# One PSUM ring for both layers of a two-mixture network, and attention scores of two heads in the two halves of the array's rows

## The chip, the cores and the metric

One NeuronCore of a Trainium2 chip runs the whole program. Its engines work side by side, each in the order of its own instruction stream: TensorE (PE, with its weight loads as PEld), VectorE (DVE), ScalarE (ACT), GpSimd (POOL) and SyncE (SP), which issues most DMAs. The metric is the device time of one execution in microseconds (us); lower is better.

## What is computed

The reference has three stages, one after the other.

```python
# 1. linear attention with decay: 4 batches, 8 heads, 768 tokens, 48 values a head
for t in range(S):
    cur = einsum('bhd,bhe->bhde', u[None] * k_t, v_t)
    y[:, :, t] = einsum('bhd,bhde->bhe', r_t, state + cur)
    state = w[None, :, :, None] * state + einsum('bhd,bhe->bhde', k_t, v_t)
# x: 3072 tokens of 384 values
# 2. first mixture, 4 experts, each token passes all of them (p: normalised weights)
out = sum over e of p[:, e:e+1] * (relu(x @ w1[e]) @ w2[e])      # 384 -> 1024 -> 384
# 3. second mixture, 8 experts; each token goes to one, by a greedy assignment over all
#    3072 x 8 gate logits, largest first, at most 384 tokens an expert
out[mask_e] = relu(x[mask_e] @ w1[e]) @ w2[e]
```

Everything is float32 in and out.

## The kernel before

**Precision.** A float32 product of the mixtures is made as three products in the type fp32r: each factor is written as a high part and a low part (ACT casts the high part, POOL or DVE subtracts it to get the low part), and high by high, high by low and low by high are added in PSUM.

**Units.** The first mixture runs in 32 units: four batches, four experts, two blocks of 384 tokens. A unit is `up` and then `down`. `up` has eight steps f; each makes nine products of 128x128 by 128x384 (L672, L674, L676) into one PSUM buffer, then ACT writes relu of it as the high part of h (L680) and DVE the low part (L681). `down` has three steps i of 24 products each (L693, L695, L697) and one DVE eviction (L939 or L941). `up` takes its buffers from a ring of two named l1, `down` from a ring of two named l2, and all else from a ring of four named at: eight buffers in all. The second mixture uses the same `up` and `down`, one expert after another, while the search for the next expert's tokens runs on DVE and PE in between.

**Attention chunks.** A chunk is 128 tokens of one batch, all eight heads; there are 24. The first six are done ahead of the units and in the first one, with plain float32 products for the scores (L556: one product for a head, 48 rows of the array, rows 0 to 47 for one head of a pair and 64 to 111 for the other). The other 18 are done one to a unit, in units 1 to 6 of each group of eight, and have `split_scores` set. Chunk work is a list of steps in `queue`. `tick`, called three times in a step of `up` and eight times in a step of `down`, takes a step from the queue each third time, so one step of the list follows each step f of `up`. The order for these 18 chunks before: mul (POOL, L492), k_parts (DVE cast L533, POOL difference L534), r_parts for the even heads and r_parts for the odd ones (each a DVE cast L539 and a DVE difference L540 on 64 partitions), pre (POOL: L498, L502, L506), pre2 (DVE reduction cc, L517, which needs L502; POOL L523), scores of the first two pairs (L549 to L551), att (scores of the other two pairs, then two DVE maskings, L562), yy (products L579 and L583, then DVE L590), state (L600) and tr (L616). The last three fall into `down`.

**How the scores of a pair are made.** Rb holds r of a pair of heads in a block-diagonal form: 256 columns, the even head's r in rows 0 to 63 of the first 128 columns, the odd head's in rows 64 to 127 of the last 128, zeros elsewhere. So one product over all 128 rows with 256 columns gives the scores of both heads, and three of them make a pair. The zeros are written once, at the start (L643).

**Which unit loads what.** In units of block 1, w1 of the next expert is split beside `up`, two parts at odd f; in units of block 0, w2, one part at each f (ACT L658, then POOL L659). Every unit with a chunk has one or the other. All of these share ACT's and POOL's order with the chunk's steps.

Of the kernel before, what the change touches and what calls it, by code (L numbers as in the profile page):

```python
# [8 lines left out]
F32 = mybir.dt.float32  # L9
# [8 lines left out]
class Route:  # L18
    """Greedy assignment, one expert filled per phase; tokens lie [128, NT]."""

# [7 lines left out]
    def consts(self):  # L28
        """Steps."""
        nc, tile, NT, E, NC = self.nc, self.tile, self.NT, self.E, self.NC  # L30
        steps = []
# [25 lines left out]
        for l, sh in enumerate(self.shift):  # L57
            v.tensor_scalar(self.G[:, l], gi, sh, None, op0=OP.logical_shift_left)
        # thresholds of the first digit, as float bits
        self.thr0 = tile([128, self.width[0] - 1], I32, "thr0")  # L60
# [3 lines left out]
        v.tensor_tensor(self.thr0, self.thr0, first, op=OP.bitwise_xor)  # L64
        # the worth of a digit, for each expert
        d = iota([E, E], "W0", F32, [[1, E]], mult=-1)
# [17 lines left out]
        self.tt = iota([128, NT, 16], "tt", BF, [[1, NT], [0, 16]])  # L84
        # rep[(v,a), (b,a')] = (a == a') * (1 if v == 0 else 128)
        r = iota([32, 128], "repi", I32, [[1, 128]], mult=-1, base=32)
# [7 lines left out]
        v.tensor_scalar(self.rep, self.rep, pf, None, op0=OP.mult)  # L94
        # bm[(b,a), (k,b')] = (b == b')
        b = iota([128, NC // 8, 8], "bmi", I32, [[0, NC // 8], [-16, 8]], mult=1)
# [3 lines left out]
        self.m = tile([128, NT], F32, "m")  # L100
        # two tiles of tokens make one product: their experts in columns from 0 and from 32
        self.ch2 = tile([128, NT // 2, 2, 32], BF, "ch")
# [8 lines left out]
    def phase(self, last, done, split=None):  # L111
        """Two lists of steps; done(idx [128, cap/128] int32, ev [128, 1] int32) is called when both are known."""
        nc, tile, pst, NT, E, NC = self.nc, self.tile, self.pst, self.NT, self.E, self.NC
# [81 lines left out]
        def rest():  # L195
            # every token left goes to the expert left
            v.tensor_reduce(m, L, axis=AX.X, op=OP.max)
            fl = tile([128, 2, NT], F32, "fl")
            v.memset(fl[:, 1], 0.0)
            v.tensor_scalar(fl[:, 0], m, -1e29, None, op0=OP.is_ge)  # L200
            scan(fl)
            s["ev"] = self.left
# [75 lines left out]

        # Each step with its time on the tensor engine and the time until the next step's operands are there.
        # The second list makes the row numbers and may run beside the next phase's search.  # L280
        tail = [(spread, 0, 1.2), (weigh, 0, 0.6), (gather, 0.78, 0.2), (index, 0.23, 0.35)]
# [13 lines left out]
def rwkv_moe_moe(ctx, tc, A, out):  # L295
# [14 lines left out]

    # The chunked form scales by powers of the decays up to the 128th, both ways; decays with which those
    # could leave the range of float32 take the step by step form instead.
    wcol = const("wcol", [128, 4], A["w"])
# [32 lines left out]
    with tc.tile_pool(name="psum0", bufs=1, space=bass.MemoryType.PSUM) as psum, tc.manual_schedule():  # L346
# [10 lines left out]
        nc.gpsimd.iota(jp, pattern=[[1, 128]], base=0, channel_multiplier=-1)  # L357
        # the tensor engine's clock rises while it is busy
        for _ in range(22):
# [5 lines left out]

        # tp[0][i] = w^(i - 64), tp[1][j] = w^(63 - j)
        def scan(p):
# [34 lines left out]
def main(ctx, tc, A, out, C, stepwise):  # L402
# [28 lines left out]
    def step_by_step():  # L431
        """x, token after token, to memory: partition (quarter of the values, b, h), state [keys, 12 values]."""
        T = 4
# [44 lines left out]

    # ---- attention
    st = {}  # L480
# [4 lines left out]
    def attn_steps(ck, detail=False):  # L485
# [42 lines left out]

        # Both factors of the scores as sums of two parts that one pass carries exactly;
        # r of a pair of heads lies apart, so that one product makes both heads' scores.  # L530
        def k_parts():
# [3 lines left out]

        def r_parts(s):
            t, n = ld[ck]
            q, cs = slice(64 * s, 64 * s + 64), slice(128 * s, 128 * s + 128)
            nc.vector.tensor_copy(Rb[q, 0, :, cs], t[q, 0])  # L539
            nc.vector.tensor_sub(Rb[q, 1, :, cs], t[q, 0], Rb[q, 0, :, cs].bitcast(F32))  # L540

        def scores(p0, p1):
            t, n = ld[ck]
            if p0 == 0:
                ps[ck] = [psum.tile([128, 4, 128], F32, name="at", bufs=4) for _ in range(2)]
            if split_scores:
                for p in range(p0, p1):
                    o = ps[ck][p // 2][:, 2 * (p % 2):2 * (p % 2) + 2, :]
                    nc.tensor.matmul(o, Kb[:, 0, p], Rb[:, 0, p], start=True, stop=False)  # L549
                    nc.tensor.matmul(o, Kb[:, 0, p], Rb[:, 1, p], start=False, stop=False)  # L550
                    nc.tensor.matmul(o, Kb[:, 1, p], Rb[:, 0, p], start=False, stop=True)  # L551
                return
            for p in range(p0, p1):
                for s in range(2):
                    q = slice(64 * s, 64 * s + 48)
                    nc.tensor.matmul(ps[ck][s][:, p, :], t[q, 1, p, :], t[q, 0, p, :], start=True, stop=True)  # L556
# [16 lines left out]
        def y_mm():  # L573
            t, n = ld[ck]
            v = n[:, 384:768]
            y = psum.tile([128, D], F32, name="at", bufs=4)
            for p in range(4):
                if c:
                    nc.tensor.matmul(y[:, 96 * p:96 * p + 96], t[:, 0, p, :], S[ck - 1][:, p, :],  # L579
                                     start=True, stop=False)  # L580
                for s in range(2):
                    h = 2 * p + s
                    nc.tensor.matmul(y[:, 48 * h:48 * h + 48], st[ck][:, p // 2, 2 * (p % 2) + s, :] if split_scores else st[ck][:, s, p, :],  # L583
                                     v[:, 48 * h:48 * h + 48],
                                     start=not c, stop=bool(s) or not c)
            st[ck] = y
# [46 lines left out]
        if not split_scores:  # L633
            return [lambda: (mul(nc.vector), pre()), pre2, lambda: scores(0, 2), att, yy, state, tr]
        return [lambda: mul(nc.gpsimd), k_parts, lambda: r_parts(0), lambda: r_parts(1), pre, pre2, lambda: scores(0, 2), att, yy, state, tr]

    if not stepwise:
        Rb = at.tile([128, 2, 4, 256], F32R, name="Rb")
        Kb = at.tile([128, 2, 4, 128], F32R, name="Kb")
        for s in range(2):  # L640
            q, cs = slice(64 * s, 64 * s + 64), slice(128 - 128 * s, 256 - 128 * s)
            for a in range(2):
                nc.scalar.activation(Rb[q, a, :, cs], C["zero"][q, :, None].to_broadcast([64, 4, 128]), AF.Copy)  # L643

    # ---- weights
    W1, W2 = {}, {}
# [14 lines left out]

    # ---- one pass of one expert over 384 tokens
    def up(xT, c0, after1, before1, tick, tick1=lambda: None, place=None, H=None):
        H = [] if H is None else H
        for f in range(FB):
            before1(f)
            p = psum.tile([128, D], F32, name="l1", bufs=2)
            w = W1[f]
# [18 lines left out]
    def down(H, evict, tick, tick1=lambda: None):  # L687
        for i in range(3):
            ts = slice(128 * i, 128 * i + 128)
            p = psum.tile([128, D], F32, name="l2", bufs=2)  # L690
            for f in range(FB):
# [13 lines left out]
    def dots(a, to):  # L705
        """a [128, D] with each column of the gate, to to [128, E2]."""
        def lg(e):
# [4 lines left out]

    # The logits of the last tokens don't wait for their rows: what the last expert adds to them is
    # h @ (W2 @ gate), so the search for the first expert to fill runs beside the products h @ W2.
    late, hv, gated = [], [], {}
# [88 lines left out]

    # first weights and first chunks
    def consts_in():
# [13 lines left out]
    else:  # L820
# [8 lines left out]
        def warm(n):  # L829
            p = psum.tile([128, 128], F32, name="l1", bufs=2)  # L830
            b = C["busy"].to_broadcast([128, 128])
            for _ in range(n):
                nc.tensor.matmul(p, b, b, start=True, stop=True)
# [158 lines left out]
    while lq:  # L992
        lq.pop(0)()
    # ---- second mixture: one expert after the other, in the order in which they fill
    search, number = [], []
# [5 lines left out]
    def start_job(idx, ev):  # L1001
# [4 lines left out]
        def load(which, src, q):  # L1006
            t = wk.tile([128, 2, D], F32, name="raw", bufs=4)
            d = nc.sync.dma_start(t, src[bass.ds(e, 1), :, 768 * q:768 * q + 768].rearrange("o p n -> p (o n)"))
            if jb["n"] == 0 and which == 1 and q == 2:
                # the rows, waited for, pass before the weights that aren't needed yet  # L1010
                tc.add_manual_dep(d.ins, jb["rows"].ins.name,
# [81 lines left out]
    def keep_warm(n):  # L1093
        p = psum.tile([128, 128], F32, name="l1", bufs=2)
        for _ in range(n):
            nc.tensor.matmul(p, route.tri, route.tri, start=True, stop=True)
# [125 lines left out]
```

## Time and profile before

| what | value |
|---|---|
| time, median of 3 runs | 1343.05 us (1341.25 to 1346.93) |
| profiled execution, span | 1348.0 us (no other time is given for it) |
| PE busy | 1257.2 us, 93% of the span |
| PEld busy | 1196.1 us, 89% |
| DVE busy | 756.8 us, 56% |
| ACT busy | 336.9 us, 25% |
| POOL busy | 579.1 us, 43% |
| HBM traffic | 83 GB/s over the span |

The span runs from the first to the last instruction of one profiled execution. Busy times of PE are those of pipelined products, so a product's listed duration is longer than the distance between two of them. The profiled execution is 0.4% above the median of the runs.

### The profile page before, as it was taken

To read this page: it belongs to the slowest core of one execution; us is meant where nothing else is said; L and a number is where in the kernel's file an instruction comes from. 1 tells how busy PE (TensorE), PEld (TensorE's weight loads), DVE (VectorE), ACT (ScalarE), POOL (GpSimd) and SP (SyncE) were. 2 spreads that over 40 slices of the span, in tenths; PEclk is the share of its full clock that TensorE was granted. 3 is DMA by queue.
4 is the path that set the end of the run, shared out by engine and by line. 5 is a ranking of instruction groups with operands and counts; after the bars stand their busy time and mean duration, and the time that the engine had idled before them with its cause. 6 is when DMAs were issued, how large, how long until landed. Compare 5 with 4: busy or idle time off the path is not lost.

```text
span 1348.0 us, 20834 instructions
## 1 busy us (share of the span) xinstructions
PE 1257.2 (93%) x7988; PEld 1196.1 (89%) x7988; DVE 756.8 (56%) x1891; ACT 336.9 (25%) x738; POOL 579.1 (43%) x557
## 2 busy tenths in 40 slices
PE   9999999999999999999999999999997798788897
PEld 8999999999999999999989999999986677666797
DVE  6644444465444446544444663877567778767621
ACT  1322222212222221122222113222303223323252
POOL 5565444402555550055555203332205545555583
PEclk6999999999999999999999999999997999989999
DMA  6342222112222220222221011231013423333351
GB/s 232 127 145 72 91 86 91 51 39 88 79 83 82 83 71 24 95 82 93 83 84 35 19 65 48 82 106 47 1 36 113 128 77 109 107 97 89 106 169 45
DMA packets 39469, 113.36 MB, mean 84 GB/s; under 512 B 5056, under 2 KB 9280, under 8 KB 39232
## 3 DMA queue, kind: packets, MB, share of 16 engines
q1 hardware_dynamic: 36288, 102.50, 23.3%
q0 software_dynamic: 3072, 9.44, 2.1%
q8 instruction: 64, 1.05, 0.3%
q14 instruction: 45, 0.37, 0.1%
HBM read 102.48 MB, written 9.44 MB: 83 GB/s over the span
## 4 chain that ended last, share of the span: by engine, by line
PE 73%; DVE 18%; issue 2%; POOL 2%; ACT 1%; another core or an unknown queue 1%; DMA 0%; POOLq 0%; SPq 0%; ACTq 0%
PE l L693 12%; PE l L695 11%; PE l L697 11%; PE l L672 9%; PE l L674 8%; PE l L676 8%; DVE Rb L540 4%; DVE h L681 4%; PE at L583 3%; POOL w L659 2%; DVE thr L187 2%; DVE Rb L539 2%; DVE oh L129 2%; PE at L579 2%; DVE scr L709 2%
## 5 line engine op out<-in xcount | busy, mean ns | idle before, releaser
L659 POOL TENSOR_TENSOR w<-raw,w 128x384 fp32r<-128x384 f32 x332 | 355.4, 1090 | 615.9 <-ACT w L658 603.9
L672 PE MATMUL l<-xT,w 128*128 128x384 f32 x960 | 334.4, 348 | 37.6 <-DVE h L681 37.0
L674 PE MATMUL l<-xT,w 128*128 128x384 f32 x960 | 326.9, 340 | 0.0
L676 PE MATMUL l<-xT,w 128*128 128x384 f32 x960 | 326.5, 340 | 0.0
L693 PE MATMUL l<-w,h 128*128 128x384 f32 x939 | 324.7, 346 | 0.0
L697 PE MATMUL l<-w,h 128*128 128x384 f32 x939 | 318.5, 339 | 0.0
L695 PE MATMUL l<-w,h 128*128 128x384 f32 x939 | 317.8, 338 | 0.4 <-POOL w L659 0.4
L680 ACT ACTIVATE h<-l 128x384 fp32r<-128x384 f32 x313 | 154.0, 492 | 639.2 <-PE l L676 597.7
L681 DVE SCALAR_TENSOR_TENSOR h<-l,h 128x384 fp32r<-128x384 f32 x313 | 171.2, 553 | 184.2 <-ACT h L680 183.5
L672 PEld LDWEIGHTS l<-xT,w 128*128 128x128 f32 x960 | 183.3, 191 | 56.6 <-DVE h L681 54.4
L674 PEld LDWEIGHTS l<-xT,w 128*128 128x128 f32 x960 | 183.5, 191 | 0.5
L676 PEld LDWEIGHTS l<-xT,w 128*128 128x128 f32 x960 | 183.1, 191 | 0.1
L695 PEld LDWEIGHTS l<-w,h 128*128 128x128 f32 x939 | 177.2, 189 | 1.4 <-POOL w L659 0.7
L693 PEld LDWEIGHTS l<-w,h 128*128 128x128 f32 x939 | 177.3, 189 | 1.0
L697 PEld LDWEIGHTS l<-w,h 128*128 128x128 f32 x939 | 177.1, 189 | 0.8
L658 ACT ACTIVATE w<-raw 128x384 fp32r<-128x384 f32 x336 | 163.7, 517 | 42.3 <-DMA raw<-in_v_dram 37.5
L709 DVE SCALAR_TENSOR_TENSOR scr<-acc,wg 128x384 f32<-128x384 f32 x192 | 104.8, 583 | 0.2
L941 DVE SCALAR_TENSOR_TENSOR acc<-l,dp,acc 128x384 f32<-128x384 f32 x72 | 44.4, 617 | 106.0 <-PE l L697 105.8
L1028 POOL DMA_INDIRECT acc<-x2d,idx x24 | 23.7, 987 | 81.3 <-DVE idx L269 76.3
L618 ACT ACTIVATE xT<-at 128x384 fp32r<-128x384 f32 x24 | 11.8, 492 | 180.1 <-PE at L616 173.0
L540 DVE TENSOR_TENSOR Rb<-rkT,Rb 64x512 fp32r<-64x512 f32 x36 | 52.4, 1456 | 1.2
L146 PEld LDWEIGHTS <-ch 128*40 128x40 bf16 x588 | 21.5, 104 | 34.8 <-DVE oh L129 21.4
(227 smaller groups left out, 1222.9 us busy)
## 6 DMA issues: line engine op xcount, KB each, us to landing
raw<-in_w_dram SPq DMA_DIRECT2D x104, 384.0 KB, 4.4
raw<-in_v_dram SPq DMA_DIRECT2D x64, 384.0 KB, 3.2
rkv<-in_rkv_dram SPq DMA_DIRECT2D x22, 640.0 KB, 4.1
rkT<-in_rkT_dram SPq DMA_DIRECT2D x22, 512.0 KB, 3.5
x2d<-acc SPq DMA_DIRECT2D x24, 192.0 KB, 1.8
wg<-in_wg_dram SPq DMA_DIRECT2D x1, 1536.0 KB
w2r<-in_w_dram SPq DMA_DIRECT2D x8, 192.0 KB, 3.2
xT<-in_rkv_dram SPq DMA_DIRECT2D x2, 640.0 KB, 10.4
```

Of the source, the lines that this page charges most:

```text
L540: nc.vector.tensor_sub(Rb[q, 1, :, cs], t[q, 0], Rb[q, 0, :, cs].bitcast(F32))
L658: nc.scalar.activation(w[:, 0], r, AF.Copy)
L659: engine.tensor_tensor(w[:, 1], r, w[:, 0].bitcast(F32), op=OP.subtract)
L672: nc.tensor.matmul(p, w[:, 0, ks], xh, start=(k == 0), stop=False)
L674: nc.tensor.matmul(p, w[:, 0, ks], xl, start=False, stop=False)
L676: nc.tensor.matmul(p, w[:, 1, ks], xh, start=False, stop=(k == 2))
L680: nc.scalar.activation(h[:, 0], p, AF.Relu)
L681: nc.vector.scalar_tensor_tensor(h[:, 1], p, 0.0, h[:, 0].bitcast(F32), op0=OP.max, op1=OP.subtract)
L693: nc.tensor.matmul(p, h[:, 0, ts], w[:, 0], start=(f == 0), stop=False)
L695: nc.tensor.matmul(p, h[:, 0, ts], w[:, 1], start=False, stop=False)
L697: nc.tensor.matmul(p, h[:, 1, ts], w[:, 0], start=False, stop=(f == FB - 1))
L709: nc.vector.scalar_tensor_tensor(scr[e % 2], x, 1.0, wg[:, e], op0=OP.mult, op1=OP.mult, accum_out=to[:, e:e + 1])
```

## The change

The two rings l1 and l2 become one ring mm of four buffers that `up` and `down` take from in turn. For the 18 chunks with `split_scores`, the block-diagonal form of r goes: Rb has 128 columns a pair, the even head's r in rows 0 to 63 and the odd head's in rows 64 to 127, and each head has its own products over 64 rows with 128 columns, the two heads in turn, into two PSUM buffers. The high part of r is cast by ACT, the low part made by one DVE difference over 128 partitions, and the two steps r_parts become one, so every later step of the chunk comes one step earlier. The zero fills go. The scores of even heads now lie in one tile and of odd heads in the other, as in the first six chunks. The rest of the diff takes out comments.

```diff
-        def r_parts(s):
+        def r_parts():
             t, n = ld[ck]
-            q, cs = slice(64 * s, 64 * s + 64), slice(128 * s, 128 * s + 128)
-            nc.vector.tensor_copy(Rb[q, 0, :, cs], t[q, 0])
-            nc.vector.tensor_sub(Rb[q, 1, :, cs], t[q, 0], Rb[q, 0, :, cs].bitcast(F32))
+            nc.scalar.activation(Rb[:, 0], t[:, 0], AF.Copy)
+            nc.vector.tensor_sub(Rb[:, 1], t[:, 0], Rb[:, 0].bitcast(F32))
...
             if split_scores:
                 for p in range(p0, p1):
-                    o = ps[ck][p // 2][:, 2 * (p % 2):2 * (p % 2) + 2, :]
-                    nc.tensor.matmul(o, Kb[:, 0, p], Rb[:, 0, p], start=True, stop=False)
-                    nc.tensor.matmul(o, Kb[:, 0, p], Rb[:, 1, p], start=False, stop=False)
-                    nc.tensor.matmul(o, Kb[:, 1, p], Rb[:, 0, p], start=False, stop=True)
+                    for n, (a, b) in enumerate(((0, 0), (0, 1), (1, 0))):
+                        for s in range(2):
+                            q = slice(64 * s, 64 * s + 64)
+                            nc.tensor.matmul(ps[ck][s][:, p, :], Kb[q, a, p], Rb[q, b, p], start=n == 0, stop=n == 2)
                 return
...
-                    nc.tensor.matmul(y[:, 48 * h:48 * h + 48], st[ck][:, p // 2, 2 * (p % 2) + s, :] if split_scores else st[ck][:, s, p, :],
+                    nc.tensor.matmul(y[:, 48 * h:48 * h + 48], st[ck][:, s, p, :],
...
-        return [lambda: mul(nc.gpsimd), k_parts, lambda: r_parts(0), lambda: r_parts(1), pre, pre2, lambda: scores(0, 2), att, yy, state, tr]
+        return [lambda: mul(nc.gpsimd), k_parts, r_parts, pre, pre2, lambda: scores(0, 2), att, yy, state, tr]
...
-        Rb = at.tile([128, 2, 4, 256], F32R, name="Rb")
+        Rb = at.tile([128, 2, 4, 128], F32R, name="Rb")
         Kb = at.tile([128, 2, 4, 128], F32R, name="Kb")
-        for s in range(2):
-            q, cs = slice(64 * s, 64 * s + 64), slice(128 - 128 * s, 256 - 128 * s)
-            for a in range(2):
-                nc.scalar.activation(Rb[q, a, :, cs], C["zero"][q, :, None].to_broadcast([64, 4, 128]), AF.Copy)
...
-            p = psum.tile([128, D], F32, name="l1", bufs=2)
+            p = psum.tile([128, D], F32, name="mm", bufs=4)
...
-            p = psum.tile([128, D], F32, name="l2", bufs=2)
+            p = psum.tile([128, D], F32, name="mm", bufs=4)
```

The first of the last two hunks is in `up`, the second in `down`; the two places that issue small products on constants (L830, L1094) change from l1 to mm in the same way.

## Rows read from the trace of the kernel before

**Rows 1.** Page: shares of the chain by engine, then the group of h's casts.
```profile
PE 73%; DVE 18%; issue 2%; POOL 2%; ACT 1%; another core or an unknown queue 1%; DMA 0%; POOLq 0%; SPq 0%; ACTq 0%
...
L680 ACT ACTIVATE h<-l 128x384 fp32r<-128x384 f32 x313 | 154.0, 492 | 639.2 <-PE l L676 597.7
```

**Rows 2.** Windows (length; busy us and count by engine; clock): three units; units 26 to 29.
```profile
145.51:178.35 32.84, 30.90 (x192) 30.22 (x192) 14.96 (x23) 7.73 (x17) 16.76 (x14) 1.00 0.25 85
178.35:210.44 32.09, 30.90 (x192) 30.22 (x192) 14.20 (x23) 7.74 (x17) 16.51 (x14) 1.00 0.26 86
274.47:299.43 24.96, 24.96 (x145) 24.96 (x145) 17.26 (x57) 3.94 (x8) 0.00 (x0) 1.00 0.07 25
835.35:942.30 106.95, 103.29 (x578) 99.43 (x577) 85.50 (x243) 29.73 (x66) 36.70 (x32) 1.00 0.24 74
```

**Rows 3.** Waits of PE (us, times, longest) in 75:780, 780:1008 and 1008:1348.
```profile
PE l L672 <- DVE h L681: 28.3, 36, 1.1
...
PE l L672 <- DVE h L681: 3.2, 7, 1.2
...
PE l L672 <- DVE h L681: 5.4, 5, 1.8
```

**Rows 4.** Timeline of PE (start, duration, what, [idle before <- releaser]), unit from 145.51.
```profile
153.13 0.34 PE L676 MATMUL l<-xT,w 128*128 128x384 f32 x1
154.59 0.44 PE L672 MATMUL l<-xT,w 128*128 128x384 f32 x1 [1.12 <-DVE h L681]
154.87 0.34 PE L674 MATMUL l<-xT,w 128*128 128x384 f32 x1
```

**Rows 5.** Timeline of DVE, the same unit.
```profile
151.38 0.98 DVE L539 CAST Rb<-rkT 64x512 fp32r<-64x512 f32 x1
152.40 1.67 DVE L540 TENSOR_TENSOR Rb<-rkT,Rb 64x512 fp32r<-64x512 f32 x1
153.99 0.54 DVE L681 SCALAR_TENSOR_TENSOR h<-l,h 128x384 fp32r<-128x384 f32 x1
...
158.62 0.55 DVE L517 TENSOR_REDUCE cc<-rkv 128x8 f32<-128x384 f32 x1 [0.94 <-POOL rkv L502]
...
162.43 0.68 DVE L562 TENSOR_TENSOR am<-at,mask 128x512 f32<-128x512 f32 x1
```

**Rows 6.** Groups by form (count | busy us, mean ns): the low parts of r.
```profile
L540 DVE TENSOR_TENSOR Rb<-rkT,Rb 64x512 fp32r<-64x512 f32 x36 | 52.4, 1456 | 1.2
```

**Rows 7.** Timeline of PE: scores of 256 columns, then the next product of up.
```profile
158.95 0.28 PE L549 MATMUL at<-Rb,Kb 128*128 128x256 f32 x1
...
159.66 0.34 PE L672 MATMUL l<-xT,w 128*128 128x384 f32 x1
159.84 0.34 PE L674 MATMUL l<-xT,w 128*128 128x384 f32 x1
```

**Rows 8.** Timeline of PE: float32 scores in two row halves; float32 products over all rows.
```profile
68.73 0.34 PE L697 MATMUL l<-w,h 128*128 128x384 f32 x1
69.00 0.71 PE L556 MATMUL at<-rkT 48*128 48x128 f32 x8
69.64 0.45 PE L693 MATMUL l<-w,h 128*128 128x384 f32 x1
69.92 0.34 PE L695 MATMUL l<-w,h 128*128 128x384 f32 x1
...
102.78 1.03 PE L600 MATMUL at<-rkv 128*128 128x96 f32 x8
```

**Rows 9.** The instructions of L556 (duration ns least/median/most, first and last start).
```profile
L556 PE MATMUL at<-rkT x64: 272/272/579, 6.3 to 71.9; 48*128 48x128 f32 x64
```

**Rows 10.** Timeline of POOL, the unit from 145.51.
```profile
153.48 2.60 POOL L659 TENSOR_TENSOR w<-raw,w 128x384 fp32r<-128x384 f32 x2
...
157.57 1.02 POOL L502 TENSOR_TENSOR rkv<-rkv,u_b 128x384 f32<-128x384 f32 x1
...
159.79 1.99 POOL L659 TENSOR_TENSOR w<-raw,w 128x384 fp32r<-128x384 f32 x2
```

More of the change, by code (lines that the diff above doesn't have):

```diff
@@ L829, in warm @@
         def warm(n):
-            p = psum.tile([128, 128], F32, name="l1", bufs=2)
+            p = psum.tile([128, 128], F32, name="mm", bufs=4)
             b = C["busy"].to_broadcast([128, 128])
@@ L1093, in keep_warm @@
     def keep_warm(n):
-        p = psum.tile([128, 128], F32, name="l1", bufs=2)
+        p = psum.tile([128, 128], F32, name="mm", bufs=4)
         for _ in range(n):
```

## The prediction

> **What bounds the kernel now.** I read the page's chain of waits first: PE carries 73% of the span and DVE 18% [rows 1], so whatever DVE takes off PE counts, and whatever is taken off DVE alone counts only where PE waits for it. Next the windows, one unit at a time. A unit without attention takes 24.96 us and PE is busy all of it; a unit with a chunk takes 32.84 us where it is of block 1 and 32.09 us where it is of block 0, and in both PE is busy 30.90, that is 1.9 and 1.2 us less than the unit lasts, at full clock (1.00) [rows 2]. Then PE's waits by stage: in the stretch that holds the 18 chunks, PE waited 28.3 us in 36 waits, two a chunk, and all of them are the first product of an `up` step waiting for DVE's eviction L681; later there are 7 such waits of 3.2 us and, in the second mixture, 5 of 5.4 us [rows 3].
>
> The timelines show why. The reader should see at 153.13 the last product of step f=4 and at 154.59 the first of f=5: 1.46 us where products otherwise follow each 0.17, and the next one comes 0.28 after it [rows 4]. DVE had cast and subtracted r of the even heads, from 151.38 to 154.07, before it came to L681 at 153.99 [rows 5] (spans overlap a little in DVE's pipeline). The eviction came late, the ring of two l1 buffers has room for one step only, PE stood still. The second r step does the same again three products later.
>
> **1. The ring of four.** A wait costs more than its idle time: in the rows shown 1.46-0.17 = 1.29 us and 0.28-0.17 = 0.11 for the restart, 1.40 for a listed idle of 1.12, so 0.28 more [rows 4]. For the 36 waits of the chunks that is 28.3+36x0.28 = 38.4 us [rows 3]; by unit 1.94+0.56 = 2.5 us in block 1 and 1.19+0.56 = 1.75 in block 0 [rows 2]. A step lasts nine products, 9x24.96/144 = 1.56 us [rows 2]. With two buffers, a step's buffer is needed again one step after it ends, with four, three steps, 4.7 us. An eviction needs ACT 0.49 [rows 1], DVE 0.54 [rows 5] and the 0.17 that the last product goes on, about 1.2, so the room grows from 0.4 to 3.5 us. The longest thing left in DVE's way is one r difference of 1.5 to 1.7 us [rows 5, 6]: all 38.4 us go. `down` loses nothing by sharing: its buffers come up again after three other tiles, and its eviction is one DVE instruction.
>
> **2. r in one step.** DVE loses two casts like that of 0.98 and one of two differences of 1.46 a chunk (about 3 us of its 15 in a unit [rows 2, 5, 6]); the cast goes to ACT, which is busy 7.7 us of a unit [rows 2] and whose 384-element casts take 0.49 [rows 1], so about 0.65 for 512. Price on PE: nothing, covered by the ring's 3.5 us; with the old ring it would be part of the old wait. The difference over 128 partitions instead of 64 I take at 1.46, what half the partitions cost now [rows 6]. The zero fills go from the start, where PE and DVE do other things: nothing.
>
> **3. The scores.** Before, six products of 256 columns take 159.66-158.95 = 0.71 us a block, and the product after them follows at 0.18: no loss at the edges [rows 7]. Two blocks a chunk, 36 in all. After, a block is 12 products of 128 columns on 64 rows. No fp32r product of 128 columns or on part of the rows is in this trace. The nearest row is the float32 form of the same scores in row halves: eight instructions, 0.71 us with the last one's 0.27, so 0.063 apart [rows 8, 9]. At the edges it costs: 0.27 from the product before to the first (0.10 over the usual), 0.20 from the last start to the next product, and 0.28 to the one after. From 68.73 to 69.92 is 1.19, less two usual distances 0.84, which is 8x0.063+0.34 [rows 8]. So 12x0.063+0.34 = 1.10 a block, 0.39 more than now, x36 = +13.9 us. The Trainium skill, TensorEngine Tiling (Array Packing), Tiling Modes (Key Properties), says that a change of tiling mode drains the engine; the 0.27 before and 0.20 after [rows 8] agree, and that rule alone speaks against making the block so short.
>
> Bounds of this term. Lowest: the halves share everything. 384 columns take 0.173 and 256 take 0.118 [rows 4, 7], so 128 take 0.064 in one half and 0.032 a product with two; 12x0.032 is 0.39 without edges and 0.73 with them: -11.5 to +0.7 us. High: the halves don't share weight loads. Float32 products over all rows with short columns are (1.03-0.27)/7 = 0.109 apart, if the last lasts as long as in rows 9, whatever lies behind it [rows 8]; 12x0.109+0.34 = 1.65, +34 us. Also high: a 128-column fp32r product costs what a float32 one costs, two instructions, 0.126 in shared halves: 1.85, +41 us. Highest: that, and the halves not sharing: 0.252, 3.36 a block, +95 us. I take 0.063, since the row has the same columns, the same alternation of halves and one load for each instruction. The Trainium skill, TensorE: Matmul & The Clock Gate, LDWEIGHTS (loading the stationary operand), prices a load by its columns alone, 128 over 1.2 GHz, an estimate of 107 ns for half the rows as for all; by it alone 24 loads a chunk would give about the +34 us, while Part 3 there (Packing small matmuls, The mechanism) lets loads into other rows overlap, which the 0.063 [rows 8, 9] bears out for float32.
>
> **4. Steps one earlier: a wait that moves.** pre2 now follows f=4, and its reduction cc stands in DVE's order before the evictions of f=5 and f=6 and the two maskings. cc waits for POOL's L502: in the block 1 unit that ended at 158.59 [rows 10]. Of POOL's order before it only the contention goes: two splits beside the r steps took 2.60, later ones 1.99 [rows 10], so L502 ends near 158.0. PE, without stalls: f=4's last product at 153.13, f=5 done at 154.9, scores 156.0, f=6 157.5, att 158.6, f=7 160.2; now yy comes there, not three products into `down`. DVE: cc to 158.6, eviction of f=5 to 159.1, of f=6 to 159.65, maskings of 0.68 [rows 5] to 160.95. The y products need the second masking some 0.4 after they start, at 160.6, since even and odd heads now lie in two tiles: 0.4 us of wait, 1.0 if L502 is as late as before; I take 0.5. In block 0 units one split fewer is ahead of L502 and the maskings end before PE comes: nothing, with some 2 us of cover in POOL. 9x0.5 = +4.5 us. Behind the waiting cc are evictions, which the ring covers; behind the waiting y product all of PE. Note that this wait shrinks as the scores grow and the reverse.
>
> **5. Later stages.** Units 26 to 29 take 106.95, 7.1 more than four plain units; DVE is busy 85.5 of it [rows 2]. PE's seven waits there are worth 3.2+7x0.28 = 5.2 [rows 3] and the ring should take most of the loss: between 0 and 7.1, I take 5. In the second mixture only five waits of 5.4+5x0.28 = 6.8 us [rows 3] can go, and the search runs on DVE and PE in turn, which would then wait elsewhere: 0 to 6.8, I take 2.
>
> **Sum.** -38.4+13.9+4.5-5-2 = -27.0 us on a span of 1348.0, of which nothing outside is listed; that execution lies 0.4% above the median of the runs. The terms are counted instructions and waits, so I take them off the median: 1343.05-27.0 = 1316.
>
> **The rivals.** (a) The halves share nearly all, and the scores cost 0.4 to 0.7 a block: no drain worth the name. Then PE reaches the y products up to 1.4 us earlier and waits for the same cc: about 1.1 to 1.8 us x9 = 10 to 16. -38.4+0.7+10-7 = -35 or -38.4-11.5+16-7 = -41: 1302 to 1308, I say 1306. For: float32 halves share already [rows 9]. Against: the edges in rows 8. The Trainium skill, TensorEngine Tiling (Array Packing), Overview (Theoretical Speedup), promises up to 2x for a contraction of 64 or less; by that rule this case would come.
> (b) Loads are not shared: -38.4+34-7 = -11, 1332. Or 128 columns are priced as float32: -38.4+41-7 = -4, 1339. In both the wait at the y products is gone, the scores being longer than it. For: nothing in the trace has fp32r under 256 columns. Against: 0.063 in rows 9.
> (c) The other side: priced as float32 and one half after the other, 3.36 a block: -38.4+95-7 = +50, 1393. Without the scores and the wait that they replace, the change gives 45.4 us, 1.26 a block; the scores turn it into a loss from 0.71+1.26 = 1.97 a block, 0.136 a product. Rows 8 stand at 0.063, so it takes twice that.
> (d) The change doesn't do what it says, in that cc takes the place of r: POOL a microsecond later than I think gives 2.0 us in each block 1 unit, 18 instead of 4.5, and 1330. For: POOL has no gap before L502 in block 1 [rows 10]. Against: contention goes down.
>
> **How the numbers follow.** Forecast 0.44 (1316, own range 1307 to 1326); (a) 0.10; (b) 0.28, half for each price; (c) 0.07; (d) 0.11. A measurement can tell about 0.5%, 6.7 us. Faster is below 1336.3: the forecast, (a), most of (d) (0.09), most of the first half of (b) (0.10) and the near end of the second (0.04): 0.77. Same: the rest of (d) and of (b) but 0.01, 0.15. Slower: (c) and that 0.01: 0.08. Range 1304 to 1341: (c), the far part of the second price of (b) (0.06) and the far end of (a) (0.04) are left out, under 0.2.
>
> **What would show it.** The windows: units of block 1 near 31.6 us and of block 0 near 31.1. PE's waits L672 on L681 gone before 780 us. Twelve scores 0.063 apart with 0.27 ahead of them. Waits of L583 on the masking L562, in block 1 only, under 1 us each. DVE's cc idle over 2 us for L502. Wrong would be: L672 waits left over, score products over 0.1 apart, waits of L583 in all chunks, or a second mixture that moves by more than 5 us.

## The result and the profile after

The changed kernel took 1312.03 us (median of 4 runs, 1309.02 to 1314.98) against 1344.99 for the kernel before in its 4 runs: ratio 0.9761, interval [0.9737, 0.9786]. 1316 was forecast, and faster. The profiled executions have spans of 1348.0 and 1313.2 us, 34.8 apart. Cut at the starts of units, which the first product of `up` marks:

| stretch | before | after | difference | forecast |
|---|---|---|---|---|
| start and unit 0 | 81.45 | 79.74 | -1.7 | 0 |
| units 1 to 22, all 18 chunks | 678.95 | 652.49 | -26.5 | -20.0 |
| unit 23 | 24.96 | 24.96 | 0.0 | 0 |
| units 24 to 29 | 156.94 | 153.84 | -3.1 | -5 |
| from unit 30: end of the first mixture, the second | 405.70 | 402.17 | -3.5 | -2 |

The windows of the kernel after, in the columns of [rows 2]: the two units with a chunk that answer to those rows, units 26 to 29, then units 1 to 22.

```profile
141.11:172.11 31.00, 31.00 (x205) 30.31 (x205) 12.07 (x20) 8.24 (x18) 15.83 (x14) 1.00 0.27 90
172.11:203.02 30.91, 30.91 (x204) 30.23 (x204) 11.19 (x20) 8.25 (x18) 15.69 (x14) 1.00 0.27 90
807.11:911.03 103.92, 102.05 (x578) 101.08 (x578) 87.17 (x243) 29.39 (x66) 37.31 (x32) 0.98 0.26 77
...
79.74:732.23 652.49, 652.11 (x4183) 639.36 (x4183) 280.36 (x609) 164.10 (x356) 283.20 (x261) 1.00 0.24 79
```

In a unit with a chunk PE is now busy as long as the unit lasts. DVE has about 3 us less a unit, ACT 0.5 more. The page shows the same from its chain, where PE had 73% and DVE 18% [rows 1]:

```profile
PE 79%; DVE 11%; POOL 4%; issue 4%; ACT 1%; DMA 0%; POOLq 0%; SPq 0%; DVEq 0%
```

PE's waits from 75 to 780 us, 28.3 us before [rows 3], are one row:

```profile
PE at L582 <- DVE am L561: 0.2, 1, 0.2
```

The price of the scores is in PE's timeline, to be read as [rows 7, 8] were:

```profile
88.93 0.34 PE L671 MATMUL mm<-xT,w 128*128 128x384 f32 x1
89.19 0.89 PE L550 MATMUL at<-Rb,Kb 64*128 64x128 f32 x12
90.01 0.45 PE L667 MATMUL mm<-xT,w 128*128 128x384 f32 x1
90.30 0.34 PE L669 MATMUL mm<-xT,w 128*128 128x384 f32 x1
```

Twelve products in 0.89 us with a last one of 0.27 stand (0.89-0.27)/11 = 0.056 apart on average; how they begin is read below, with the products of one half. The edges are those of the float32 scores: 0.26 ahead, 0.28 to the second product behind. The block costs 1.37 less two usual distances, 1.02 us, where it cost 0.71.

Last, the wait that was to move. DVE and PE in the unit from 141.11:

```profile
147.10 1.04 DVE L538 TENSOR_TENSOR Rb<-rkT,Rb 128x512 fp32r<-128x512 f32 x1
148.07 0.56 DVE L676 SCALAR_TENSOR_TENSOR h<-mm,h 128x384 fp32r<-128x384 f32 x1
...
153.33 0.55 DVE L517 TENSOR_REDUCE cc<-rkv 128x8 f32<-128x384 f32 x1 [3.14 <-POOL rkv L502]
...
154.73 1.28 DVE L561 TENSOR_TENSOR am<-at,mask 128x512 f32<-128x512 f32 x2
...
155.83 0.65 PE L582 MATMUL at<-rkv,am 128*128 128x48 f32 x4
```

DVE stands 3.14 us at cc, as foreseen; the second masking ends at 156.01, and PE takes it up at that moment: four L582 that last 0.57 elsewhere last 0.65. The unit of block 1 is 0.09 us longer than that of block 0, no more. It is more in the three block 1 units with the first chunk of a batch, units 1, 9 and 17: there is no state yet, so the two products L578 ahead of the y products are missing and PE comes 0.2 us sooner. In unit 1:

```profile
94.27 0.34 PE L582 MATMUL at<-rkv,am 128*128 128x48 f32 x2
94.79 1.43 PE L582 MATMUL at<-rkv,am 128*128 128x48 f32 x11 [0.18 <-DVE am L561]
```

From the first pair to the next it is 0.52 us where it is 0.18 without a wait; each of the three units loses 0.3 to 0.4 us in this way.

### The profile page after: what moved, and what is told of

It is laid out like the page before. It is cut to its first block, busy times and chain, and to the rows that moved or that the text cites. A ratio compares the mean times of both kernels' runs of the same rounds, so it can differ in the third digit from the quotient of the medians.

```text
span 1313.2 us, 21208 instructions
## 1 busy us (share of the span) xinstructions
PE 1252.3 (95%) x8204; PEld 1195.4 (91%) x8204; DVE 708.6 (54%) x1837; ACT 343.4 (26%) x752; POOL 565.1 (43%) x557
## 4 chain that ended last, share of the span: by engine, by line
PE 79%; DVE 11%; POOL 4%; issue 4%; ACT 1%; DMA 0%; POOLq 0%; SPq 0%; DVEq 0%
PE mm L688 12%; PE mm L692 12%; PE mm L690 12%; PE mm L667 11%; PE mm L669 10%; PE mm L671 10%; PE at L582 3%; POOL w L654 3%; DVE thr L187 2%; PE at L550 2%; DVE oh L129 2%; PE at L146 2%; PE at L578 2%; DVE h L676 1%; PE at L599 1%
## 5 line engine op out<-in xcount | busy, mean ns | idle before, releaser
L654 POOL TENSOR_TENSOR w<-raw,w 128x384 fp32r<-128x384 f32 x332 | 346.5, 1063 | 601.5 <-ACT w L653 586.1
L667 PE MATMUL mm<-xT,w 128*128 128x384 f32 x960 | 332.6, 346 | 0.6 <-ACT xT L1039 0.6
L669 PE MATMUL mm<-xT,w 128*128 128x384 f32 x960 | 327.1, 341 | 0.0
L671 PE MATMUL mm<-xT,w 128*128 128x384 f32 x960 | 326.3, 340 | 0.0
L688 PE MATMUL mm<-w,h 128*128 128x384 f32 x939 | 325.1, 346 | 0.8 <-ACT w L653 0.8
L675 ACT ACTIVATE h<-mm 128x384 fp32r<-128x384 f32 x313 | 153.9, 492 | 636.9 <-PE mm L671 595.2
L690 PE MATMUL mm<-w,h 128*128 128x384 f32 x939 | 318.6, 339 | 1.1 <-POOL w L654 1.1
L692 PE MATMUL mm<-w,h 128*128 128x384 f32 x939 | 318.8, 339 | 0.0
L676 DVE SCALAR_TENSOR_TENSOR h<-mm,h 128x384 fp32r<-128x384 f32 x313 | 171.9, 553 | 176.6 <-ACT h L675 176.4
L667 PEld LDWEIGHTS mm<-xT,w 128*128 128x128 f32 x960 | 184.0, 192 | 4.7 <-ACT xT L1039 1.0
L669 PEld LDWEIGHTS mm<-xT,w 128*128 128x128 f32 x960 | 183.8, 191 | 0.6
L671 PEld LDWEIGHTS mm<-xT,w 128*128 128x128 f32 x960 | 183.5, 191 | 0.1
L690 PEld LDWEIGHTS mm<-w,h 128*128 128x128 f32 x939 | 178.0, 190 | 2.3 <-POOL w L654 1.7
L688 PEld LDWEIGHTS mm<-w,h 128*128 128x128 f32 x939 | 177.7, 189 | 2.1 <-ACT w L653 1.1
L692 PEld LDWEIGHTS mm<-w,h 128*128 128x128 f32 x939 | 177.6, 189 | 0.9
L936 DVE SCALAR_TENSOR_TENSOR acc<-mm,dp,acc 128x384 f32<-128x384 f32 x72 | 44.4, 617 | 110.2 <-PE mm L692 110.1
L146 PE MATMUL at<-oh,ch 128*40 128x62 bf16 (+2 forms) x588 | 27.3, 196 | 28.3 <-DVE oh L129 22.0
L582 PE MATMUL at<-rkv,am 128*128 128x48 f32 x352 | 51.4, 273 | 0.4 <-DVE am L561 0.2
```

What stands on the lines that cost most here:

```text
L582: nc.tensor.matmul(y[:, 48 * h:48 * h + 48], st[ck][:, s, p, :], v[:, 48 * h:48 * h + 48], start=not c, stop=bool(s) or not c)
L654: engine.tensor_tensor(w[:, 1], r, w[:, 0].bitcast(F32), op=OP.subtract)
L667: nc.tensor.matmul(p, w[:, 0, ks], xh, start=(k == 0), stop=False)
L669: nc.tensor.matmul(p, w[:, 0, ks], xl, start=False, stop=False)
L671: nc.tensor.matmul(p, w[:, 1, ks], xh, start=False, stop=(k == 2))
L675: nc.scalar.activation(h[:, 0], p, AF.Relu)
```

## The experiments

Ratios are to the kernel before on the same chip, with their intervals. Runs with one number were made once, for their profile.

**The ring alone.** The kernel before, with this edit at the four places that used l1 or l2:

```diff
-            p = psum.tile([128, D], F32, name="l1", bufs=2)
+            p = psum.tile([128, D], F32, name="mm", bufs=4)
```

> The kernel before with nothing but the ring of four. Ring theory (the four buffers remove the 36 waits of 38.4 us; the new scores only cost): units with a chunk fall to 30.3 us, no wait of L672 on L681 before 780 us, and the time is 8 to 11 us below the changed kernel's, 1301 to 1304 us. Relief theory (DVE is freed by one r step, and that removes the waits): over half of the waits stay, the time is above 1325 us.

1298.46 us, 0.9673 [0.9651, 0.9695]: faster than the whole change, and lower than the 1301 to 1304 expected. The windows of two units with a chunk and of units 1 to 22:

```profile
141.85:172.33 30.48, 30.48 (x193) 30.28 (x192) 15.46 (x23) 7.73 (x17) 16.67 (x14) 1.00 0.26 92
172.33:202.62 30.29, 30.29 (x192) 30.25 (x192) 14.13 (x23) 7.74 (x17) 16.52 (x14) 1.00 0.28 91
...
81.89:723.77 641.88, 641.86 (x3967) 639.27 (x3967) 335.41 (x663) 155.04 (x338) 298.71 (x261) 1.00 0.24 81
```

DVE still does the two r steps (15.46 us of the unit, 14.96 before), and no wait of PE is listed. Units 1 to 22 are 678.95-641.88 = 37.1 us shorter: the four buffers alone take all the waits. Against the whole change, 652.49-641.88 = 10.6 us, near 36 blocks of 0.31, 11.2. (The agreement is not exact: this kernel's own block 1 units are 0.2 to 0.3 us longer than those of block 0, at the first products of a block of scores, about 2 us in all, and the change has the waits at the y products instead.)

**The change without the ring.** The changed kernel with l1 and l2 of two buffers again, the edit above backwards.

> The changed kernel with two rings of two again. Ring theory: with one step of room the evictions that now stand behind cc (3.1 us idle on DVE in block 1 units) stop PE by about 2 us in block 1 units and under 1 us in block 0 units; with 11 us of dearer scores the time is within 7 us of the kernel before, 1338 to 1350 us. Relief theory: the waits are gone with the r steps, 1315 to 1325 us.

1317.12 us, 0.9816 [0.98, 0.9833], which is what the relief theory said. Waits from 75 to 740 us, then a block 1 unit, units 26 to 29 and units 1 to 22:

```profile
PE l L667 <- DVE h L676: 3.2, 9, 0.5
```

```profile
143.36:174.71 31.35, 31.02 (x204) 30.23 (x204) 12.08 (x20) 8.24 (x18) 15.85 (x14) 1.00 0.26 89
812.10:919.19 107.09, 103.28 (x577) 99.46 (x577) 85.00 (x243) 29.70 (x66) 37.23 (x32) 1.00 0.25 75
...
81.99:737.13 655.14, 651.90 (x4184) 638.76 (x4184) 279.84 (x609) 164.09 (x356) 283.58 (x261) 1.00 0.24 79
```

Nine waits of 3.2 us in all are left of 28.3 [rows 3], all in block 1 units. So neither theory holds by itself: either half of the change takes nearly all the waits, and the second to come finds little. Two things were overlooked. The one r difference fits between two evictions (147.10 to 148.14 in the kernel after, the next eviction at 148.07). And the evictions behind cc have more room than one step: the two blocks of scores lie between f=5 and f=7, so a buffer of two is needed again 1.56+2x1.02 = 3.6 us after its step. The ring still gives 655.14-652.49 = 2.7 us here, all in block 1 units (about 0.35 in each of six; in units 1, 9 and 17, where the changed kernel waits at the y products instead, 0.0 to 0.25), and 107.09-103.92 = 3.2 in units 26 to 29.

**The old r steps under the new scores.** Two rings of two, scores in halves, and

```diff
-        def r_parts():
+        def r_parts(s):
             t, n = ld[ck]
-            nc.scalar.activation(Rb[:, 0], t[:, 0], AF.Copy)
-            nc.vector.tensor_sub(Rb[:, 1], t[:, 0], Rb[:, 0].bitcast(F32))
+            q = slice(64 * s, 64 * s + 64)
+            nc.vector.tensor_copy(Rb[q, 0], t[q, 0])
+            nc.vector.tensor_sub(Rb[q, 1], t[q, 0], Rb[q, 0].bitcast(F32))
...
-        return [lambda: mul(nc.gpsimd), k_parts, r_parts, pre, ...
+        return [lambda: mul(nc.gpsimd), k_parts, lambda: r_parts(0), lambda: r_parts(1), pre, ...
```

> Scores in row halves, but two rings of two and the two r steps of before (a DVE cast and a DVE difference each). Theory that the r steps made the waits and that their merging alone removes them: about 36 waits of L667 on L676 are back in the units with a chunk, these take 0.6 us more than before, 32.6 and 33.4 us less up to 0.5, and the time is 1.000 to 1.008 of before. Rival (the scores in halves changed the room of the evictions, and that removed the waits): no waits, 0.98 of before as with the merged step.

1355.67 us, 1.0088 [1.0065, 1.0111]. The waits from 75 to 750 us and two units:

```profile
PE l L668 <- DVE h L677: 27.0, 35, 1.1
```

```profile
146.84:180.19 33.35, 31.53 (x204) 30.16 (x204) 15.53 (x23) 7.72 (x17) 16.65 (x14) 1.00 0.25 84
180.19:212.90 32.71, 31.51 (x205) 30.19 (x204) 14.22 (x23) 7.73 (x17) 16.49 (x14) 1.00 0.26 85
```

They are back, 35 of 27.0 us (the 36th falls just behind 750 us), and the units are 0.5 to 0.6 us longer than before [rows 2]. So it is the merged step, not the halves, that does it in the kernel without the ring; and the new scores alone are a loss, of 0.9%. The merged step is three things at once, the cast moved to ACT, one difference in place of two and all later steps one earlier; no run separates them.

**Both heads' products in turn.** Three products of one head, then three of the other:

```diff
-                    for n, (a, b) in enumerate(((0, 0), (0, 1), (1, 0))):
-                        for s in range(2):
+                    for s in range(2):
+                        for n, (a, b) in enumerate(((0, 0), (0, 1), (1, 0))):
```

> The changed kernel with the three products of one head in a row, then those of the other, so that two neighbours are mostly in the same half of the rows. Theory of shared loads (neighbours in different halves overlap their weight loads, and that makes the 0.06 us distance): products in the same half stand 0.107 apart, a block grows by 0.35 to 0.5 us, the time by 8 to 18 us less up to 3 us of waits. Rival (0.064 us is what 128 columns take in any order, on the line through 256 columns at 0.118 and 384 at 0.173): distance and time unchanged.

1307.76 us, 0.9747 [0.9731, 0.9763]: no change. The block:

```profile
92.73 0.89 PE L550 MATMUL at<-Rb,Kb 64*128 64x128 f32 x12
```

That could mean that halves don't matter, or that three still pair with three. The next two tell.

**128 columns over all rows, and over one half.** The score product with `Kb[:, a, p]` and `Rb[:, b, p]` in place of `Kb[q, a, p]` and `Rb[q, b, p]`; and the changed kernel with `q = slice(0, 64)` for both heads.

> The changed kernel with every score product over all 128 rows, still 128 columns: the two heads of a pair are summed, so the scores are not the reference's; only its times count. Theory of shared halves (two products in different halves run beside each other; the kernel with the halves in turn could still pair up three with three): without halves the products stand 0.107 apart, a block takes 1.3 us or more against 1.02. Rival (128 columns take 0.056 in any rows): same distance of 0.056, a block of 0.7 to 1.0 us.

> The changed kernel with both heads' score products on rows 0 to 63 (the odd head's scores are those of the even head; only its times count). Theory of shared halves: one half has all the work, 0.107 apart, a block of 1.6 us with the edges, units 1.1 to 1.2 us longer than the changed kernel's. Rival (0.056 in any rows): unchanged units.

1324.86 and 1338.6 us. All rows first, then one half:

```profile
122.16 0.33 PE L671 MATMUL mm<-xT,w 128*128 128x384 f32 x1
122.33 1.45 PE L550 MATMUL at<-Rb,Kb 128*128 128x128 f32 x12
123.62 0.39 PE L667 MATMUL mm<-xT,w 128*128 128x384 f32 x1
123.85 0.34 PE L669 MATMUL mm<-xT,w 128*128 128x384 f32 x1
```

```profile
122.06 0.34 PE L671 MATMUL mm<-xT,w 128*128 128x384 f32 x1
122.33 1.55 PE L550 MATMUL at<-Rb,Kb 64*128 64x128 f32 x12
123.81 0.44 PE L667 MATMUL mm<-xT,w 128*128 128x384 f32 x1
124.09 0.34 PE L669 MATMUL mm<-xT,w 128*128 128x384 f32 x1
```

Over all rows the products stand (1.45-0.27)/11 = 0.107 apart on average and a block takes 1.69-0.35 = 1.34 us; in one half it is (1.55-0.27)/11 = 0.116 and 2.03-0.35 = 1.68, and the units are 1.3 to 1.4 us longer than the changed kernel's, where 1.1 to 1.2 were expected. The two averages differ by the first distance alone. From the second product on, all rows first:

```profile
122.39 1.39 PE L550 MATMUL at<-Rb,Kb 128*128 128x128 f32 x11
```

```profile
122.49 1.39 PE L550 MATMUL at<-Rb,Kb 64*128 64x128 f32 x11
```

That is (1.39-0.27)/10 = 0.11 apart in both, after a first distance of 0.06 over all rows and 0.16 in one half. So 128 columns are not free to run at 0.056 by themselves: two halves beside each other make it. The starts in the kernel with the heads in turn show how. The score products that have begun in two windows, both opened just before the block, are counted as x:

```profile
92.70:92.89 0.19, 0.16 (x2) 1.00 1.71 146
92.70:93.00 0.30, 0.27 (x4) 1.00 1.18 119
```

They begin in twos, a new two each 0.11 us, though the program has three products of one half in a row; in one half alone only one begins in that time. So three pair with three. The changed kernel's begin in twos as well. The Trainium skill, TensorE: Matmul & The Clock Gate, LDWEIGHTS (loading the stationary operand), sets 128 columns over 1.2 GHz for a load, an estimate of 107 ns; the 0.11 comes near, and Part 3 there (The mechanism), by which loads into other rows overlap, agrees with the twos. The entry of 0.27 shows only with 64 rows; over all rows it is 0.17. TensorEngine Tiling (Array Packing) of the Trainium skill, Tiling Modes (Key Properties), has a drain at a change of mode, and these entries agree.

**One block of scores.** All four pairs after f=5, the maskings where the second block was:

```diff
-        return [..., pre2, lambda: scores(0, 2), att, yy, state, tr]
+        return [..., pre2, lambda: scores(0, 4), am, yy, state, tr]
```

> The changed kernel with the scores of all four pairs in one block of 24 products after f=5, none after f=6. Theory of the edges (each block pays 0.34 us for entering and leaving the row halves, whatever its length): one block a chunk less, units 0.3 us shorter, the time 5 to 7 us less. Rival (the cost is in the products): units unchanged, the time within 2 us.

1319.16 us, 0.9762 [0.973, 0.9794], no gain; the units got longer, 31.2 us in both blocks. The block and the y products of one unit:

```profile
121.48 1.55 PE L550 MATMUL at<-Rb,Kb 64*128 64x128 f32 x24
122.96 0.44 PE L667 MATMUL mm<-xT,w 128*128 128x384 f32 x1
...
126.59 0.42 PE L582 MATMUL at<-rkv,am 128*128 128x48 f32 x2
127.19 0.42 PE L582 MATMUL at<-rkv,am 128*128 128x48 f32 x2 [0.18 <-DVE am L561]
```

The edges are what I took them for: 24 products in one block, again 0.056 apart, cost 1.68 us, 0.36 less than two of 1.02. But f=6 and f=7 now follow each other, the maskings wait for the eviction of f=6, and PE reaches them too early: 0.60 from one pair of L582 to the next and a wait at each of two maskings. The saving and 0.2 to 0.3 us more went there.

**One block, maskings at once.** The same, with `lambda: (scores(0, 4), am())` for the two steps, which also brings the y products one step earlier.

> The changed kernel with the scores of all pairs in one block and the two maskings in the same step, ahead of the eviction of f=6. Theory (one block saves 0.36 us of edges, and the one-block kernel lost it again because its y products came to the maskings too early): units of 30.55 us in block 0, 0.36 less than the changed kernel's, no wait of L582, the time 5 to 7 us under the one-block kernel in units 1 to 23. Rival (one block costs elsewhere): units stay at 31.2 us.

1329.71 us, 0.9911 [0.9883, 0.9939]: half right. A block 0 and a block 1 unit, two stretches of the latter, and the waits from 75 to 750:

```profile
177.43:208.01 30.58, 30.58 (x204) 30.23 (x204) 11.40 (x20) 8.25 (x18) 16.05 (x14) 1.00 0.28 91
208.01:243.30 35.29, 34.23 (x205) 33.59 (x204) 12.67 (x20) 8.24 (x18) 16.16 (x14) 0.90 0.24 79
...
220.60:222.80 2.20, 1.14 (x9) 0.85 (x7) 2.20 (x5) 0.49 (x1) 2.20 (x3) 1.00 0.00 0
222.80:230.50 7.70, 7.70 (x37) 7.70 (x37) 1.33 (x4) 1.31 (x3) 2.11 (x3) 0.57 0.21 70
```

```profile
PE at L582 <- DVE am L561: 10.5, 18, 1.2
```

Block 0 is the 30.58 expected. In block 1 the wait of step 4 is there in full: cc still ends when POOL lets it, the y products come 1.6 us earlier than with one block (1.9 earlier than in the changed kernel), PE is busy 1.14 us of 2.2, and in the 7.7 us after that the granted clock is 0.57 of full, mostly the lower of its two levels (1.2 instead of 2.4 GHz). Units of block 1 took 31.6 to 35.3 us.

**Fetching ahead.** In unit 26 the changed kernel takes 29.01 us, more than the 26.69 before, though L667 waits no more. SyncE's waits from 795 to 845 us, then ACT and PE in that unit:

```profile
SPq L717 <- DVE scr L704: 45.4, 4, 24.2
```

```profile
823.06 0.52 ACT L653 ACTIVATE w<-raw 128x384 fp32r<-128x384 f32 x1 [4.34 <-DMA raw<-in_w_dram]
...
823.63 0.44 PE L688 MATMUL mm<-w,h 128*128 128x384 f32 x1 [0.76 <-ACT w L653]
824.71 0.45 PE L690 MATMUL mm<-w,h 128*128 128x384 f32 x1 [0.64 <-POOL w L654]
825.99 0.69 PE L690 MATMUL mm<-w,h 128*128 128x384 f32 x1 [0.48 <-POOL w L654]
...
829.01 0.33 PE L690 MATMUL mm<-w,h 128*128 128x384 f32 x1
```

The waits are not all of the loss. A window behind them shows the granted clock at 0.50, the lower of its two levels:

```profile
826.00:828.00 2.00, 2.00 (x6) 2.00 (x7) 2.00 (x8) 0.00 (x0) 0.00 (x0) 0.50 0.00 0
```

The nine products from 825.99 on take 3.02 us until 829.01, where 9x0.17 = 1.6 is usual: by this estimate 1.4 of the unit's 4 us went with the clock, the rest with the three waits (1.9 listed) and their restarts.

SyncE stands at a fetch of w2 rows for the gate, whose buffer DVE still reads, and the weight load of `down` is queued behind it. The edit gives those rows four buffers:

```diff
-            w[f] = rt.tile([128, D], F32, name="w2r", bufs=2)
+            w[f] = rt.tile([128, D], F32, name="w2r", bufs=4)
```

> The changed kernel with four buffers instead of two for the rows of w2 that DVE multiplies with the gate in unit 26. Theory (SyncE stands in a fetch that waits for DVE, the weight load behind it comes late, and unit 26 gives 4 us back): unit 26 falls from 29.0 to 25.0 us, and the time by 3 to 4 us. Rival (the load is late for another reason, such as its own buffers): unit 26 stays at 29 us.

1305.11 us, 0.9721 [0.97, 0.9742]. Unit 26, then units 26 to 29:

```profile
809.75:834.75 25.00, 25.00 (x146) 25.00 (x146) 21.82 (x63) 7.26 (x16) 9.19 (x8) 1.00 0.28 88
809.75:909.63 99.88, 99.88 (x578) 99.88 (x578) 84.68 (x243) 29.54 (x66) 38.69 (x32) 1.00 0.25 72
```

103.92-99.88 = 4.0 us, all of what PE had left to lose there, the clock's part with it (1.00). The times of the whole kernel agree, but their intervals touch those of the kernel after; the units are the evidence.

**Ring and fetch, old scores.** The ring alone, with that edit.

> The kernel before with the ring of four and four buffers for the rows of w2, its scores in the block-diagonal form: the version that the runs so far point to. Theory (the scores in halves cost 0.31 us a block, 11 us in all; the fetch 3 to 4 us more): 0.3% below the ring alone, 0.963 to 0.965 of before, 1291 to 1297 us, units 26 to 29 of 24.96 to 25.2. Rival (the halves cost nothing and the ring alone was fast for another reason, such as the second mixture): no better than 0.967.

1297.12 us, 0.9618 [0.9591, 0.9645], the fastest of all, 1.5% under the change by their ratios. Units 26 to 29, 104.29 us with the ring alone, and units 1 to 22:

```profile
796.94:897.76 100.82, 100.33 (x577) 99.78 (x577) 85.71 (x243) 29.52 (x66) 38.38 (x32) 1.00 0.25 71
...
79.50:722.06 642.56, 642.55 (x3967) 639.77 (x3967) 334.48 (x663) 154.91 (x338) 299.03 (x261) 1.00 0.24 80
```

Unit 27 took 25.91 us, over the 25.2 expected: one wait on an eviction, of 0.5 us, is left there.

## Why the prediction was right, point by point

- **The waits (-38.4).** All went, as forecast; with the ring alone units 1 to 22 give 37.1. The forecast put them down to the ring and said that the r step, with the old ring, would be part of the old wait. That was wrong, without harm to the sum: with the old ring and the merged step 3.2 us of listed waits are left, and with the old steps 27.0. Of the two halves either would have done.
- **r in one step (0).** Right for PE: ACT's extra cast is in no wait. The difference over 128 partitions took 0.89 us on average (1.04 in the unit shown), below the 1.46 taken for it.
- **The scores (+13.9).** The edges of 0.34 a block were right; the products stand 0.056 apart on average, not 0.063, so a block is 1.02 instead of 1.10 and the term, with the wait of the next point, 10.6 against the ring alone. The bound on loads that aren't shared (0.109) is what the runs without two halves give (0.11), and fp32r at 128 columns does not cost what float32 costs, so rivals (b) and (c) are out. Rival (a), no drain, is out too, by its block of 0.4 to 0.7; the time alone would not have told, since 1312 lies between its 1306 and the forecast's 1316.
- **The wait that moves (+4.5).** Over-sized: 0.09 us in six block 1 units and 0.3 to 0.4 in the three that begin a batch, which the forecast did not set apart: about 1.5 us in all. POOL's L502 ended 12.2 us into the unit, against 12.5 foreseen, and the maskings ended as PE arrived. The mechanism was right, and the experiment with the maskings at once shows it with 10.5 us of listed waits when PE comes 1.9 us sooner; the change has no room there. That a later POOL would have cost as much, rival (d), is likely from this but was not run.
- **Units 24 to 29 (-5).** -3.1: the ring took the stalls on DVE, but the step that failed is the idea that nothing else comes due. A weight load, late behind SyncE's fetch, became the next wait in unit 26 and cost 4 us of it, 1.4 by the lower clock behind it.
- **Start (0) and from unit 30 on (-2).** -5.2 together, but these stretches differ from kernel to kernel where nothing in them was changed: the start lasts 79.4 to 83.3 us, and the part from unit 30 394.5 with ring and fetch, 399.4 with the ring alone. The five waits on evictions of [rows 3], 5.4 us, are gone in the second mixture, but PE's listed waits from unit 30 on fell only from 45.9 to 43.9 us: it waits more for the search, as feared. What of the 3.5 us belongs to the ring is not settled.

The total was forecast at -27.0; the medians give -33.0, the two spans -34.8. From -27.0 to -34.8: scores and y wait cost 7.8 less, the waits gave 1.3 less, the start and the second mixture 3.2 more, units 24 to 29 1.9 less.

## What to carry to other kernels

When one engine's lateness stalls another, more buffers and less work on the late engine are two cures for one stall: price them apart, and count the gain once. Half the rows does not mean half the time: here two products of 128 columns, one in each half, took 0.11 us together, and the block-diagonal product of 256 columns that they replaced took 0.118, so there was little to gain, and the 0.34 us at the edges of each block made it a loss. After a stall is gone, look at what its slack had been covering: here a load queued behind a fetch, and a masking that PE now reaches just in time.

## What the runs showed of the hardware that was not expected

- fp32r products of 128 columns follow each other 0.11 us apart, over all 128 rows and in one half of 64 rows alike; if two halves share them, two begin in each 0.11 us (0.056 on average), whether the halves alternate one by one or three by three.
- Moving from products over all rows to products over 64 rows costs 0.10 us at entry; over all rows, with the same 128 columns, there was none.
- After a stretch of 2.2 us in which PE was busy 1.14 us, the granted clock was 0.57 over the next 7.7 us. In unit 26 of the changed kernel it was 0.50 from 826 to 828 us, behind waits of 0.76, 0.64 and 0.48 us. In the kernel before, with waits of up to 1.1 us in the chunk units, it stayed at 1.00 [rows 2, 3].
